# Float16 halves for the scores of a pooled-attention MLP kernel, and DMA-turned queries and values

## The chip, the core and the metric

The kernel runs on one core of one Trainium2 chip. The metric is the device time of one execution in microseconds, lower is better. TensorE (PE) multiplies matrices, VectorE (DVE), ScalarE (ACT) and GpSimd (POOL) work on tiles of 128 partitions, and SyncE (SP) issues all DMAs of this kernel, in order, on one queue. Each engine works through its own list of instructions in the order in which the program wrote them, and waits at semaphores for the others.

## The reference

Four batches of 12288 queries of 128 channels; `kv` is 384 x 32 positions of 128 channels per batch. Keys and values are the same pooled matrix.

```python
kv_pool = kv.reshape(B, H // r, r, W // r, r, C).mean(axis=(2, 4))   # r = 4: 768 positions
kv_flat = kv_pool.reshape(B, -1, C) @ w_sr
k = v = kv_flat
s = scale * (q @ k.transpose(0, 2, 1)); s = s - s.max(-1, keepdims=True)
a = np.exp(s); a /= a.sum(-1, keepdims=True) + 1e-09
x = (a @ v).reshape(B * N, C)
h = x @ w_in                                  # 128 -> 2048
g = 0.5 * h * (1.0 + erf(h / sqrt(2)))
out = g @ w_out                               # 2048 -> 128
```

## The kernel before

**Tiles.** The 49152 tokens are 96 tiles of 512, 24 to a batch. A tile has four token blocks `c` of 128. To keep float32 precision on 16-bit or reduced matmuls, each operand is split into a high and a low half, and three products (high-high, high-low, low-high) are added in PSUM.

**Stages of a tile t**, with the lines that the profile names:

- `q_load`; `q_planes` (L307) copies the upper and lower 16 bits of q apart, `q_turn` lets a DMA transpose these two planes, `q_join` (L321) puts them together, `q_high` (L335) and `q_low` (L341) make the two float32r halves. All on GpSimd in the steady loop but `q_high`, which is on VectorE.
- `score` (L352): for each block, six matmuls of 384 columns (three products, two halves of the 768 keys) into the one buffer `ps_s`. `evac` (L363) copies it to SBUF times -1.0 and takes the minimum.
- `exps` (L409, ScalarE), `recips` (L422, L425), then `attn` per block: `attn_hi` (L429) and `attn_lo` (L433) on VectorE, and `attn_turn` (L442), a DMA transpose into `aT`, of which there is one buffer.
- `av` (L471): 18 matmuls of 512 columns with the value halves. `x_out` (L481, L482) splits the result.
- For each of 16 blocks `f` of the hidden layer: `mlp_in` (L490 to L492), `gelu` (L504, and L506 for each pair, which makes `gh`), `rest` (L510, VectorE, makes `gl` for a pair), `mlp_out` (L521 to L523), six steps later. The pair's float32 result `g` has two buffers, so the gelu of a pair waits for the `rest` of the pair two before.
- The output is copied into 16-bit planes (`o_turn`, L307), turned by DMA, joined (`o_join`) and stored.

**Order.** Nothing is scheduled by a planner: the program writes the order by hand. `START` lists the work of the start and of tile 0. After it a double loop over tile i and step f mixes the MLP of tile i with the attention of tiles i+1 to i+3: `q_load(i+3)` at f=1, blocks 1 to 3 of `attn(i+1)` at f=1, 3, 5, `score` and `evac` of tile i+2 at f=3, 6, 9, q's planes and turn at f=5, its join at f=8, `exps(i+2)` and q's halves at f=10, `av(i+1)` at f=10 to 12, `score(i+3, 0)` at f=13, `recips(i+2)` and block 0 at f=15, and a `rest` at every even f. Within one f the order of the source holds.

**Keys and values.** Each batch's keys are summed, turned on TensorE (`kv_turn`, L201), multiplied by `w_sr` (`kv_key`) and split (`kv_key_low`, L220). When all are there, each channel's largest gives a scale; the scaled keys are turned back on TensorE (`kv_val`, L286) and split into the value halves. `mlp_scale` needs the largest over the partitions: a matmul with ones (L249) and a reduction.

**Weights.** `w_max`, `w_scale` and `w_split` make float16 halves of both weights in the start, with scales per partition.

Of the kernel before, what the change touches and what calls it, by code (L numbers as in the profile page):

```python
# [23 lines left out]
    ("q_planes", 0, "act"), ("kv_load", 3), ("kv_load", 4), ("kv_load", 5), ("q_load", 1),  # L24
    ("q_turn", 0), ("kv_load", 6), ("kv_load", 7), ("q_planes", 1, "pool"), ("kv_load", 8),
    ("kv_load", 9), ("kv_load", 10), ("kv_load", 11), ("wi_load", 0), ("wi_load", 1), ("q_turn", 1),
    ("q_load", 2), ("q_load", 3), ("wo_load", 0), ("wi_load", 2), ("wo_load", 1), ("wi_load", 3),
# [1 line left out]
    ("kv_sum", 1, 1), ("kv_sum", 2, 0), ("kv_sum", 2, 1), ("kv_key_low", 0), ("kv_turn", 1),
    ("kv_key", 1), ("kv_turn", 2), ("q_join", 0, "act"), ("q_high", 0, "act"), ("q_low", 0),  # L30
# [6 lines left out]
    ("kv_turn", 5), ("w_max", 2), ("w_max", 3), ("w_scale", 0), ("kv_key", 5), ("kv_key_low", 5), ("evac_half", 0, 3, 0), ("w_split", 0, 2),
    ("kv_max",), ("w_split", 1, 0), ("q_join", 1, "act"), ("w_split", 0, 3),
    ("score_half", 0, 0, 1), ("evac_half", 0, 0, 1), ("exp", 0, 0), ("score_half", 0, 1, 1),
    ("evac_half", 0, 1, 1), ("evac_half", 0, 2, 0), ("exp", 0, 1), ("score_half", 0, 2, 1),  # L40
    ("evac_half", 0, 2, 1), ("kv_scale", 0), ("exp", 0, 2), ("recips", 0, 0, 2), ("kv_scale", 1),
    ("score_half", 0, 3, 1), ("q_high", 1, "pool"), ("q_low", 1), ("q_join", 2, "pool"),
    ("kv_mul",), ("mlp_scale",), ("recips", 0, 2, 1), ("evac_half", 0, 3, 1), ("attn_hi", 0, 0, "act"),
    ("attn_hi", 0, 1, "act"), ("exp", 0, 3), ("attn_hi", 0, 2, "act"), ("attn_lo", 0, 0),
    ("attn_turn", 0, 0), ("attn_lo", 0, 1), ("attn_turn", 0, 1), ("recips", 0, 3, 1),
    ("w_split", 1, 1), ("attn_hi", 0, 3, "act"), ("attn_lo", 0, 2), ("attn_turn", 0, 2),
    ("attn_lo", 0, 3), ("attn_turn", 0, 3), ("q_planes", 3, "act"), ("w_max", 4),
# [7 lines left out]
    ("score_half", 1, 3, 1), ("score", 1, 2), ("mlp_in", 0, 0), ("evac_half", 1, 1, 1),
    ("exp", 1, 1), ("evac", 1, 2), ("exp", 1, 2), ("evac_half", 1, 3, 0), ("evac_half", 1, 3, 1),
    ("exp", 1, 3), ("q_high", 2, "act"), ("q_low", 2), ("w_split", 2, 1), ("recips", 1, 0, 4),
    ("w_split", 2, 2), ("attn_hi", 1, 0, "act"), ("attn_lo", 1, 0), ("attn_turn", 1, 0),
    ("q_turn", 3), ("attn_hi", 1, 1, "act"), ("gelu", 0, 0), ("w_split", 2, 3), ("score", 2, 0),
    ("mlp_in", 0, 1), ("attn_lo", 1, 1), ("evac", 2, 0), ("gelu", 0, 1), ("w_split", 5, 0),  # L60
    ("attn_turn", 1, 1), ("mlp_in", 0, 2), ("gelu", 0, 2), ("w_split", 5, 1), ("rest", 0, 0),
    ("w_split", 5, 2), ("w_split", 5, 3), ("score", 2, 1), ("mlp_in", 0, 3),
    ("attn_hi", 1, 3, "act"), ("gelu", 0, 3), ("attn_hi", 1, 2, "act"), ("w_split", 3, 0),
    ("mlp_in", 0, 4), ("w_split", 3, 1), ("evac", 2, 1), ("rest", 0, 1), ("attn_lo", 1, 3),
    ("attn_lo", 1, 2), ("attn_turn", 1, 2), ("gelu", 0, 4), ("mlp_in", 0, 5), ("gelu", 0, 5),
    ("w_split", 3, 2), ("attn_turn", 1, 3), ("w_split", 3, 3), ("mlp_out", 0, 0), ("mlp_in", 0, 6),
    ("mlp_out", 0, 1), ("gelu", 0, 6), ("score", 2, 2), ("rest", 0, 2), ("evac", 2, 2),
    ("mlp_in", 0, 7), ("gelu", 0, 7), ("w_split", 6, 0), ("mlp_out", 0, 2), ("mlp_in", 0, 8),
    ("mlp_in", 0, 9), ("gelu", 0, 8), ("rest", 0, 3), ("w_split", 6, 1), ("w_split", 6, 2),
    ("w_split", 6, 3), ("gelu", 0, 9), ("mlp_out", 0, 3), ("mlp_out", 0, 4), ("mlp_in", 0, 10),  # L70
    ("score", 2, 3), ("q_join", 3, "dve"), ("evac", 2, 3), ("mlp_out", 0, 5), ("av", 1, 0),
    ("gelu", 0, 10), ("exp", 2, 2), ("w_split", 7, 0), ("q_high", 3, "pool"), ("q_low", 3),
    ("exp", 2, 1), ("exp", 2, 0), ("exp", 2, 3), ("mlp_in", 0, 11), ("av", 1, 1), ("mlp_in", 0, 12),
    ("av", 1, 2), ("gelu", 0, 11), ("gelu", 0, 12), ("mlp_in", 0, 13), ("mlp_out", 0, 6),
    ("w_split", 7, 1), ("w_split", 7, 2), ("rest", 0, 4), ("x_out", 1), ("gelu", 0, 13),
    ("mlp_out", 0, 7), ("mlp_out", 0, 8), ("rest", 0, 5), ("mlp_out", 0, 9), ("score", 3, 0),
    ("mlp_in", 0, 14), ("gelu", 0, 14), ("mlp_in", 0, 15), ("recips", 2, 0, 4),
    ("attn_hi", 2, 0, "dve"), ("rest", 0, 6), ("attn_lo", 2, 0), ("gelu", 0, 15), ("evac", 3, 0),
# [5 lines left out]
def pooled_attention_mlp(  # L84
# [145 lines left out]

    def kv_scale(b, step):
        if step == 0:
            e2 = small.tile([P, 1], I32, tag="e2", name=f"e2_{b}")
# [3 lines left out]
            nc.vector.tensor_scalar(
                e2, st["mx", b].bitcast(I32), 0x7F800000, None, op0=ALU.bitwise_and
            )
# [533 lines left out]
```

## Time and profile before

| | |
|---|---|
| three runs | 2953.82, 2955.94, 2957.46 us; median 2955.94 |
| profiled execution | 2959.45 us, its span 2957.7 us |
| granted TensorE clock | 0.99 |
| busy | PE 2828.8, ACT 2535.7, DVE 2294.4, POOL 992.6 us |

The span is what the profiler saw from the first to the last instruction; the execution's time is a little longer. In the rows below, a timeline row gives start and length in us, engine, line, operation, output <- inputs, shapes and count, and in brackets how long the engine stood idle before it and what released it. A group row gives, after the count, the busy time in us and the mean of one in ns, then the idle time before them. A row of the stretches gives start and end, and for PE, PE's weight loads, DVE, ACT and POOL the busy time with the number of instructions. Names lose their buffer numbers, so `g` is any buffer of `g`.

### The profile page before, as it was taken

Reading aid. Unit: us, or ns where it says so; the run is one execution under the profiler, and the core shown is the slowest. Engines: PE = TensorE matmul, PEld = TensorE weight load, DVE = VectorE, ACT = ScalarE, POOL = GpSimd, SP = SyncE. Lnnn points to the kernel's source line nnn. Section 1 sums busy time; section 2 is a strip of 40 time slices with the busy share of each in tenths; the row PEclk is TensorE's granted clock in tenths of the full one; section 3 lists DMA queues with packets and bytes.
Section 4 is the critical chain, followed back from the end, with each engine's and each line's share of the span. In section 5 each row is a group of like instructions: output and inputs, shape, how many; then the busy total and the mean of one; then the engine's idle time right before and its main releaser. Section 6 shows DMA issues by size and latency. Waiting matters only on the chain.

```text
span 2957.7 us, 37444 instructions
## 1 busy us (share of the span) xinstructions
PE 2828.8 (96%) x13412; PEld 1479.2 (50%) x13412; DVE 2294.4 (78%) x3043; ACT 2535.7 (86%) x3429; POOL 992.6 (34%) x1009
## 2 busy tenths in 40 slices
...
GB/s 189 66 95 113 94 113 95 94 85 86 93 100 107 102 115 89 104 75 93 86 97 97 116 106 100 107 86 89 82 97 86 93 86 97 86 93 86 93 84 56
DMA packets 848443, 283.31 MB, mean 96 GB/s; under 512 B 808576, under 2 KB 811008, under 8 KB 848256
## 3 DMA queue, kind: packets, MB, share of 16 engines
...
q8 instruction: 105, 1.72, 0.2%
...
## 4 chain that ended last, share of the span: by engine, by line
PE 56%; DVE 22%; ACT 10%; issue 4%; DMA 4%; POOL 0%; SPq 0%; ACTq 0%; DVEq 0%
PE px L471 10%; DVE gl L510 9%; PE s L352 7%; PE po L521 7%; PE po L522 6%; PE po L523 6%; PE h L490 6%; PE h L492 6%; PE h L491 6%; DVE a L433 5%; DVE a L429 4%; ACT g L504 4%; DMA aT<-a 3%; ACT sn L409 3%; DVE sn L363 2%
## 5 line engine op out<-in xcount | busy, mean ns | idle before, releaser
L504 ACT ACTIVATE g<-h,hs 128x512 f32<-128x512 f32 x1536 | 1003.3, 680 | 327.1 <-DVE gl L510 160.7
L510 DVE SCALAR_TENSOR_TENSOR gl<-g,gs,gh 128x1024 f16<-128x1024 f32 x768 | 1027.4, 1347 | 129.9 <-ACT gh L506 125.9
L506 ACT ACTIVATE gh<-g,gs 128x1024 f16<-128x1024 f32 x768 | 882.1, 1149 | 24.9
L307 POOL COPY q_u<-q 128x512 uint16<-128x512 uint16 x188 | 189.4, 1035 | 1332.1 <-DMA q<-in_q_dram 1315.3
L522 PE MATMUL po<-gl,wo_h 128*128 128x512 f16 x1536 | 583.4, 380 | 8.9 <-DVE gl L510 8.9
L521 PE MATMUL po<-gh,wo_h 128*128 128x512 f16 x1536 | 586.4, 382 | 2.1 <-ACT oT L528 2.1
L490 PE MATMUL h<-xh,wi_h 128*128 128x512 f16 x1536 | 585.1, 381 | 0.1
L491 PE MATMUL h<-xl,wi_h 128*128 128x512 f16 x1536 | 583.8, 380 | 0.0
L492 PE MATMUL h<-xh,wi_l 128*128 128x512 f16 x1536 | 583.6, 380 | 0.0
L523 PE MATMUL po<-gh,wo_l 128*128 128x512 f16 x1536 | 583.3, 380 | 0.0
L433 DVE SCALAR_TENSOR_TENSOR a<-sn,r,a 128x768 f16<-128x768 f32 x384 | 426.3, 1111 | 13.3
L471 PE MATMUL px<-aT,vh 128*128 128x512 f16 x1140 | 342.9, 383 | 45.4 <-issue 32.7
L363 DVE TENSOR_SCALAR_CACHE_REDUCE sn<-s 128x768 f32<-128x768 f32 x378 | 358.6, 949 | 21.2 <-PE s L352 20.8
L409 ACT ACTIVATE sn<-sn,nm 128x768 f32<-128x768 f32 x384 | 354.5, 924 | 20.6 <-DVE nm L403 17.8
L481 DVE TENSOR_SCALAR xh<-px,xs 128x512 f16<-128x512 f32 x96 | 72.1, 751 | 366.2 <-PE px L471 366.2
L321 POOL COPY qT<-q_v 128x512 uint16<-128x512 uint16 x186 | 219.1, 1220 | 210.3 <-DMA q_v<-q_u 210.3
L352 PE MATMUL s<-kh,qh 128*128 128x384 f32 x756 | 263.8, 430 | 8.6 <-DVE sn L363 4.5
L429 DVE TENSOR_SCALAR a<-sn,r 128x768 f16<-128x768 f32 x376 | 254.7, 677 | 3.8 <-DVE r L425 0.5
L523 PEld LDWEIGHTS <-wo_l 128*128 128x128 f16 x1536 | 150.5, 98 | 191.1 <-issue 10.8
L521 PEld LDWEIGHTS <-wo_h 128*128 128x128 f16 x1536 | 150.2, 98 | 188.8 <-issue 44.8
L490 PEld LDWEIGHTS <-wi_h 128*128 128x128 f16 x1536 | 150.6, 98 | 186.5 <-issue 17.6
L492 PEld LDWEIGHTS <-wi_l 128*128 128x128 f16 x1536 | 150.7, 98 | 182.3 <-issue 1.9
...
## 6 DMA issues: line engine op xcount, KB each, us to landing
...
aT<-a SPq DMA_TRANSPOSE x384, 3.8
...
q_v<-q_u SPq DMA_TRANSPOSE x96, 3.6
o_v<-o_u SPq DMA_TRANSPOSE x95, 3.4
```

What stands on the lines that cost most here:

```text
L352: nc.tensor.matmul(ps[:, n, :KH], lhs[:, cs], rhs[:, n * KH : (n + 1) * KH], start=rhs is kh and lhs is qh, stop=lhs is ql,)
L433: nc.vector.scalar_tensor_tensor(a[:, 1, :], st.pop(("s", t, c)), st["r", t][:, c : c + 1], a[:, 0, :], op0=ALU.mult, op1=ALU.subtract,)
L471: nc.tensor.matmul(ps, v[:, k, :], aT[:, :, o + k, :], start=k == 0 and i == 0, stop=k == KB - 1 and i == 2,)
L490: nc.tensor.matmul(ps, wi_h[:, fs], xh, start=True, stop=False)
L491: nc.tensor.matmul(ps, wi_h[:, fs], xl, start=False, stop=False)
L492: nc.tensor.matmul(ps, wi_l[:, fs], xh, start=False, stop=True)
L504: nc.scalar.activation(g[:, e, :], ps, AF.Gelu, scale=st["hs", b])
L506: nc.scalar.mul(gh, g, st["gs", b])
L510: nc.vector.scalar_tensor_tensor(gl, st["g", t, p], st["gs", t // TPB], st["gh", t, p], op0=ALU.mult, op1=ALU.subtract)
L521: nc.tensor.matmul(ps, wo_h[:, f, :], gh[:, e, :], start=f == 0, stop=False)
L522: nc.tensor.matmul(ps, wo_h[:, f, :], gl[:, e, :], start=False, stop=False)
L523: nc.tensor.matmul(ps, wo_l[:, f, :], gh[:, e, :], start=False, stop=f == FB - 1)
```

## The change

- **Queries.** `q_planes`, `q_join`, `q_high` and `q_low` go. At f=4 `q_max` reduces each token's absolute largest on VectorE, `q_scale` makes a power of two and its inverse from it (three small operations), and `q_split` on GpSimd multiplies by the inverse, copies to float16 and subtracts: two float16 halves. At f=8 `q_turn` has the DMA transpose the halves, and `q_sigma` (VectorE) makes the factor that undoes the scales of token and keys. The halves go straight into the matmuls.
- **Keys.** One scale per batch: `kv_max`, and `kv_bound` in four steps (a diagonal, the matmul with ones, the reduction and the scales). `kv_high` and `kv_low` make float16 halves of all keys. `kv_key_low` and `kv_mul` go.
- **Scores.** The matmuls read float16 halves; `evac` multiplies by `q_sigma`'s column instead of -1.0.
- **Values.** `kv_val` is one DMA transpose of the key halves; the transposes on TensorE and the split of the values go.
- **MLP scales.** `mlp_scale` is three small operations per batch; the largest over the partitions is taken once, in `w_scale`, which is now in three steps. `w_split`'s third step can run on ScalarE.
- **Start.** `START` is written anew: all of the first batch's keys come first, then the four blocks of tile 0's scores, and most weight splits after the first `av`.

The core of the diff:

```diff
+    def q_max(t):
+        st["qm", t] = small.tile([P, CH], F32, tag="qm", name=f"qm_{t}")
+        nc.vector.tensor_reduce(
+            st["qm", t], st["q", t], axis=AX.X, op=ALU.max, apply_absolute_value=True)
+    def q_scale(t):
+        m = st.pop(("qm", t))
...
+        nc.vector.tensor_scalar_max(m, m, 2.0**-90)
+        nc.vector.tensor_scalar(
+            st["qe", t], m.bitcast(I32), 0x7F800000, None, op0=ALU.bitwise_and)
+        nc.vector.tensor_scalar(
+            st["qi", t], st["qe", t], -1.0, float(268 << 23), op0=ALU.mult, op1=ALU.add)
+    def q_split(t, eng=nc.gpsimd):
+        x = st.pop(("q", t))
+        u = qs.tile([P, 2, CH, C], F16, tag="u", name=f"q_{t}_u")
+        i = st.pop(("qi", t)).bitcast(F32).unsqueeze(2).to_broadcast([P, CH, C])
+        eng.tensor_tensor(x, x, i, op=ALU.mult)
+        eng.tensor_copy(u[:, 0], x)
+        eng.tensor_tensor(u[:, 1], x, u[:, 0], op=ALU.subtract)
     def q_turn(t):
-        st["qv", t] = turn(qs, st.pop(("qu", t)), f"q_{t}")
+        u = st.pop(("qu", t))
+        v = qs.tile([P, 2, CH, P], F16, tag="v", bufs=2, name=f"q_{t}_v")
+        nc.sync.dma_start_transpose(
+            v.rearrange("p e c d -> p (e c) d"), u.rearrange("p e c d -> p (e c d)"))
+        st["qT", t] = v[:, 0], v[:, 1]
+    def q_sigma(t):
+        st["sg", t] = small.tile([P, CH], F32, tag="sg", name=f"sg_{t}")
+        nc.vector.tensor_scalar_mul(
+            st["sg", t], st.pop(("qe", t)).bitcast(F32), st["ks", t // TPB])
...
-            s.rearrange("p (n k) -> p n k", n=2), st.pop(("ps", t, c))[:, :, :KH], -1.0, None,
+            s.rearrange("p (n k) -> p n k", n=2), st.pop(("ps", t, c))[:, :, :KH],
+            st["sg", t][:, c : c + 1], None,
...
+    def kv_high(b, n=0, parts=1, mul=nc.vector.tensor_scalar_mul):
+        if n == 0:
+            st["k", b] = keys.tile([P, 2, KEYS], F16, tag="k", name=f"k_{b}")
+        s = slice(n * KEYS // parts, (n + 1) * KEYS // parts)
+        mul(st["k", b][:, 0, s], st["kT", b][:, s], st["kinv", b])
+    def kv_low(b, n=0, parts=1):
...
+        nc.vector.scalar_tensor_tensor(
+            k[:, 1, s], st["kT", b][:, s], st["kinv", b], k[:, 0, s],
+            op0=ALU.mult, op1=ALU.subtract)
+    def kv_val(b):
+        st["v", b] = keys.tile([P, 2 * KB, C], F16, tag="v", name=f"v_{b}")
+        nc.sync.dma_start_transpose(st["v", b], st["k", b].rearrange("p n k -> p (n k)"))
...
-        at(i1, 11, kv_scale, b, 0)
-        at(i1, 11, kv_scale, b, 1)
-        at(i1, 11, kv_mul, b)
-        at(i1 + 1, 9, mlp_scale, b)
-        at(i1 + 1, 9, out_scale, b)
-        at(i1 + 1, 11, kv_val, b, 0, 4, ps_t, "ps_t")
...
+        at(i1, 11, kv_bound, b, 0)
+        at(i1 + 1, 2, kv_bound, b, 1)
+        at(i1 + 1, 11, kv_bound, b, 2)
+        at(i1 + 1, 11, kv_bound, b, 3)
+        at(i1 + 1, 12, mlp_scale, b)
+        at(i1 + 1, 12, out_scale, b)
+        at(i1 + 2, 11, kv_high, b)
+        at(i1 + 2, 12, kv_low, b)
+        at(i1 + 3, 11, kv_val, b)
...
-                if i + 3 < NT and f == 5:
-                    q_planes(i + 3)
-                    q_turn(i + 3)
+                if i + 3 < NT and f == 4:
+                    q_max(i + 3)
+                    q_scale(i + 3)
+                    q_split(i + 3)
+                if i + 3 < NT and f == 8:
+                    q_turn(i + 3)
+                    q_sigma(i + 3)
...
-                if f == 8 and i + 3 < NT:
-                    q_join(i + 3)
-                if f == 10 and i + 3 < NT:
-                    q_high(i + 3)
-                    q_low(i + 3)
```

In the new `START`, after the loads and the keys of the first batch:

```python
    ("kv_turn", 4), ("kv_key", 4), ("kv_turn", 5), ("kv_key", 5), ("kv_max", 1), ("kv_bound", 0),
    ("w_split", 0, 0), ("kv_bound", 1), ("w_max", 0), ("kv_bound", 2), ("kv_high", 0),
    ("kv_high", 1), ("kv_low", 0), ("kv_bound", 3), ("q_sigma", 0), ("kv_low", 1), ("kv_val",),
    ("score_half", 0, 0, 0), ("score_half", 0, 1, 0), ("score_half", 0, 2, 0),
...
    ("w_scale", 0, 0), ("w_scale", 0, 1), ("w_split", 0, 1), ("w_split", 0, 2, "act"),
    ("w_scale", 0, 2), ("mlp_scale",), ("w_split", 0, 3), ("q_sigma", 1), ("score", 1, 0),
    ("evac", 1, 0), ("score_half", 1, 1, 0), ("score_half", 1, 1, 1), ("w_split", 1, 0),
    ("av_first", 0, 0), ("av_first", 0, 1), ("w_split", 1, 1), ("w_split", 1, 2, "act"),
    ("av_first", 0, 2), ("av_first", 0, 3), ("exp", 1, 0), ("w_split", 1, 3), ("x_out", 0),
```

More of the change, by code (lines that the diff above doesn't have):

```diff
@@ L23 @@
     ("q_load", 0), ("kv_load", 0), ("kv_load", 1), ("w_sr",), ("kv_load", 2),
[L24 to L27, printed above, removed]
+    ("q_max", 0), ("q_scale", 0), ("q_split", 0), ("kv_load", 3), ("kv_load", 4), ("kv_load", 5),
@@ L28 @@
+    ("q_load", 1), ("kv_load", 6), ("q_turn", 0), ("kv_load", 7), ("kv_load", 8), ("kv_load", 9),
+    ("kv_load", 10), ("kv_load", 11), ("wi_load", 0), ("wi_load", 1), ("wi_load", 2),
+    ("wi_load", 3), ("q_load", 2), ("wo_load", 0), ("wo_load", 1),
     ("kv_sum", 0, 0), ("kv_sum", 0, 1), ("kv_sum", 1, 0), ("kv_turn", 0), ("kv_key", 0),
[L29 to L30 removed]
@@ L37 @@
[L37 to L47, printed above, removed]
@@ L55 @@
[L55 to L66, printed above, removed]
@@ L67 @@
[L67 to L78, printed above, removed]
@@ L79 @@
-    ("attn_turn", 2, 0), ("w_split", 7, 3),
+    ("kv_sum", 1, 1), ("kv_sum", 2, 0), ("kv_sum", 2, 1), ("kv_turn", 1), ("kv_key", 1),
+    ("q_max", 1), ("q_scale", 1), ("q_split", 1), ("kv_turn", 2), ("kv_sum", 3, 0),
+    ("kv_sum", 3, 1), ("kv_key", 2), ("kv_max", 0), ("kv_sum", 4, 0), ("kv_turn", 3),
+    ("kv_key", 3), ("kv_sum", 4, 1), ("q_turn", 1), ("kv_sum", 5, 0), ("kv_sum", 5, 1),
+    ("kv_turn", 4), ("kv_key", 4), ("kv_turn", 5), ("kv_key", 5), ("kv_max", 1), ("kv_bound", 0),
+    ("w_split", 0, 0), ("kv_bound", 1), ("w_max", 0), ("kv_bound", 2), ("kv_high", 0),
@@ new lines @@
+    ("score_half", 1, 3, 1), ("exp", 1, 2), ("evac_half", 1, 3, 0), ("evac_half", 1, 3, 1),
+    ("exp", 1, 3), ("recips", 1, 0, 4), ("attn_hi", 1, 0, "dve"), ("attn_lo", 1, 0),
+    ("attn_turn", 1, 0), ("gelu", 0, 0), ("mlp_in", 0, 1), ("gelu", 0, 1), ("w_max", 4),
+    ("w_max", 5), ("w_max", 6), ("w_max", 7), ("w_scale", 1, 0), ("mlp_in", 0, 2),
+    ("w_scale", 1, 1), ("gelu", 0, 2), ("rest", 0, 0), ("w_split", 4, 0), ("w_split", 4, 1),
+    ("w_scale", 1, 2), ("out_scale",), ("w_split", 4, 2, "dve"), ("w_split", 4, 3),
@@ new lines @@
+    ("mlp_in", 0, 3), ("gelu", 0, 3), ("rest", 0, 1), ("w_split", 2, 0), ("w_split", 2, 1),
+    ("w_split", 2, 2, "dve"), ("w_split", 2, 3), ("q_sigma", 2), ("score", 2, 0), ("mlp_in", 0, 4), ("evac", 2, 0),
+    ("gelu", 0, 4), ("mlp_in", 0, 5), ("gelu", 0, 5), ("rest", 0, 2), ("attn_hi", 1, 1, "dve"),
+    ("attn_lo", 1, 1), ("attn_turn", 1, 1), ("mlp_out", 0, 0), ("mlp_in", 0, 6),
+    ("mlp_out", 0, 1), ("gelu", 0, 6), ("w_split", 5, 0), ("w_split", 5, 1), ("score", 2, 1),
+    ("evac", 2, 1), ("w_split", 5, 2, "dve"), ("w_split", 5, 3), ("mlp_in", 0, 7),
@@ new lines @@
+    ("gelu", 0, 7), ("mlp_out", 0, 2), ("rest", 0, 3), ("attn_hi", 1, 2, "dve"),
+    ("attn_lo", 1, 2), ("attn_turn", 1, 2), ("mlp_out", 0, 3), ("w_split", 3, 0), ("w_split", 3, 1),
+    ("w_split", 3, 2, "dve"), ("w_split", 3, 3), ("mlp_in", 0, 8), ("gelu", 0, 8),
+    ("attn_hi", 1, 3, "dve"), ("attn_lo", 1, 3), ("attn_turn", 1, 3), ("mlp_in", 0, 9),
+    ("gelu", 0, 9), ("mlp_out", 0, 4), ("rest", 0, 4), ("score", 2, 2), ("evac", 2, 2),
+    ("mlp_out", 0, 5), ("q_max", 3), ("q_scale", 3), ("q_split", 3), ("q_turn", 3),
@@ new lines @@
+    ("q_sigma", 3), ("mlp_in", 0, 10), ("gelu", 0, 10), ("w_split", 6, 0), ("w_split", 6, 1),
+    ("mlp_in", 0, 11), ("gelu", 0, 11), ("mlp_out", 0, 6), ("rest", 0, 5), ("w_split", 6, 2, "dve"),
+    ("w_split", 6, 3), ("score", 2, 3), ("evac", 2, 3), ("mlp_out", 0, 7),
+    ("mlp_in", 0, 12), ("gelu", 0, 12), ("exp", 2, 0), ("exp", 2, 1), ("exp", 2, 2), ("exp", 2, 3),
+    ("av", 1, 0), ("w_split", 7, 0), ("w_split", 7, 1), ("mlp_in", 0, 13), ("av", 1, 1),
+    ("gelu", 0, 13), ("mlp_out", 0, 8), ("rest", 0, 6), ("av", 1, 2), ("w_split", 7, 2, "dve"),
@@ L80 @@
+    ("w_split", 7, 3), ("x_out", 1), ("mlp_in", 0, 14), ("gelu", 0, 14), ("mlp_out", 0, 9),
+    ("recips", 2, 0, 4), ("attn_hi", 2, 0, "dve"), ("attn_lo", 2, 0), ("attn_turn", 2, 0),
+    ("mlp_in", 0, 15), ("gelu", 0, 15), ("score", 3, 0), ("evac", 3, 0),
 ]
@@ L321, in join @@
             copy(w[:, :, e], v[:, e, :, :].rearrange("p c d -> p (c d)"))
-    def q_planes(t, *copy):
-        st["qu", t] = planes(qs, st.pop(("q", t)).rearrange("p c d -> p (c d)"), f"q_{t}", *copy)
-    def q_turn(t):
-        st["qv", t] = turn(qs, st.pop(("qu", t)), f"q_{t}")
-    def q_join(t, *copy):
-        st["qj", t] = qs.tile([P, T], F32, tag="qT", name=f"qT_{t}")
-        join(st.pop(("qv", t)), st["qj", t], *copy)
-    def q_high(t, copy=nc.vector.tensor_copy):
-        qh = qs.tile([P, T], F32R, tag="qh", name=f"qh_{t}")
-        copy(qh, st["qj", t])
-        st["qh", t] = qh
@@ L385, in score_half @@
         for i, (lhs, rhs) in enumerate(((qh, kh), (ql, kh), (qh, kl))):
-            nc.tensor.matmul(ps, lhs[:, cs], rhs[:, ks], start=i == 0, stop=i == 2)
+            nc.tensor.matmul(ps, lhs[:, c], rhs[:, ks], start=i == 0, stop=i == 2)
         st["s", t, c, n] = ps
```

268 lines of the change are left out of this document (138 added, 130 removed).

## The prediction

> **What bounds the kernel now.** I read the page first: busy shares and the chain that ended last.
>
> ```profile
> PE 2828.8 (96%) x13412; PEld 1479.2 (50%) x13412; DVE 2294.4 (78%) x3043; ACT 2535.7 (86%) x3429; POOL 992.6 (34%) x1009
> ...
> PE 56%; DVE 22%; ACT 10%; issue 4%; DMA 4%; POOL 0%; SPq 0%; ACTq 0%; DVEq 0%
> ```
>
> By the shares TensorE is the bound, but a quarter of the chain runs through VectorE and the transposes. So I read one quiet tile in the timelines, first VectorE from one `recips` (L422) to the next.
>
> ```profile
> 2403.01 0.16 DVE L422 TENSOR_SCALAR r<-sum 128x4 f32<-128x4 f32 x1
> ...
> 2409.87 0.62 DVE L429 TENSOR_SCALAR a<-sn,r 128x768 f16<-128x768 f32 x1
> 2410.52 1.24 DVE L433 SCALAR_TENSOR_TENSOR a<-sn,r,a 128x768 f16<-128x768 f32 x1
> 2411.69 1.63 DVE L510 SCALAR_TENSOR_TENSOR gl<-g,gs,gh 128x1024 f16<-128x1024 f32 x1
> 2413.24 0.96 DVE L429 TENSOR_SCALAR a<-sn,r 128x768 f16<-128x768 f32 x1
> 2414.24 1.24 DVE L433 SCALAR_TENSOR_TENSOR a<-sn,r,a 128x768 f16<-128x768 f32 x1
> 2415.40 0.94 DVE L363 TENSOR_SCALAR_CACHE_REDUCE sn<-s 128x768 f32<-128x768 f32 x1
> 2416.28 0.08 DVE L363 DVE_READ_ACCUMULATOR sn<-s 128x1 f32 x1
> 2416.28 2.92 DVE L510 SCALAR_TENSOR_TENSOR gl<-g,gs,gh 128x1024 f16<-128x1024 f32 x2
> ...
> 2432.52 0.16 DVE L422 TENSOR_SCALAR r<-sum 128x4 f32<-128x4 f32 x1
> ```
>
> No row from 2403.01 on names a wait: for 14.6 us, to the end of the first L510 of the last pair (about 2417.5), VectorE runs back to back. ScalarE and TensorE hang on that stretch:
>
> ```profile
> 2417.65 1.26 ACT L504 ACTIVATE g<-h,hs 128x512 f32<-128x512 f32 x2 [1.79 <-DVE gl L510]
> ...
> 2420.69 1.28 ACT L409 ACT_TABLE_LOAD   x1
> ...
> 2430.13 1.15 ACT L506 ACTIVATE gh<-g,gs 128x1024 f16<-128x1024 f32 x1
> ```
>
> ```profile
> 2418.67 0.38 PE L492 MATMUL h<-xh,wi_l 128*128 128x512 f16 x1
> 2419.37 0.59 PE L471 MATMUL px<-aT,vh 128*128 128x512 f16 x2 [0.33 <-DMA aT<-a]
> ```
>
> The gelu of f=8 needs one of the two `g` buffers, so it waits 1.79 us for that L510. From there ScalarE is busy (gelus, a table load, four exps) until `gh` at 2431.28, which releases the L510 ahead of the next `recips`. So there is a ring with no slack: 14.6 us of VectorE, 13.7 us of ScalarE, 1.2 us of L510, together 29.5. TensorE is nearly as slow but stands at `av` until the last attention transpose has landed: it has slack, the ring has none. First and last steady `recips`, 93 tiles apart:
>
> ```profile
> 160.49 0.16 DVE L422 TENSOR_SCALAR r<-sum 128x4 f32<-128x4 f32 x1
> ...
> 2901.99 0.16 DVE L422 TENSOR_SCALAR r<-sum 128x4 f32<-128x4 f32 x1
> ```
>
> (2901.99 - 160.49)/93 = 29.48 us a tile. What is put into that VectorE stretch is paid 93 times.
>
> GpSimd matters because it stretches VectorE there:
>
> ```profile
> 2410.05 2.19 POOL L307 COPY q_u<-q 128x512 uint16<-128x512 uint16 x2 [15.02 <-DMA q<-in_q_dram]
> 2412.95 1.72 POOL L307 COPY o_u<-oT 128x512 uint16<-128x512 uint16 x2 [0.71 <-ACT oT L528]
> ```
>
> Beside these copies L433 takes 1.24 us twice, L429 0.96, L510 1.63. The same lines without such a neighbour take 1.02, 0.62 and 1.28 (second fence below). That is 0.22 + 0.35 + 0.34 + 0.22 = 1.13 us a tile of sharing.
>
> **The change, part by part.** Rows that price it:
>
> ```profile
> L580 DVE TENSOR_REDUCE wm<-wi 128x1 f32<-128x512 f32 x4 | 2.7, 684 | 5.9 <-DMA wi<-in_moe_w_in_dram 5.9
> L237 DVE TENSOR_SCALAR e<-mx 128x1 int32<-128x1 int32 x4 | 0.6, 154 | 0.1
> L335 DVE CAST qh<-qT 128x512 fp32r<-128x512 f32 x92 | 38.6, 420 | 8.5 <-POOL qT L321 8.5
> L481 DVE TENSOR_SCALAR xh<-px,xs 128x512 f16<-128x512 f32 x96 | 72.1, 751 | 366.2 <-PE px L471 366.2
> L294 DVE CAST vh<-pv 128x512 f16<-128x512 f32 x4 | 2.8, 693 | 13.8 <-PE pv L286 13.8
> ```
>
> ```profile
> 2404.08 1.02 DVE L433 SCALAR_TENSOR_TENSOR a<-sn,r,a 128x768 f16<-128x768 f32 x1
> 2405.02 1.28 DVE L510 SCALAR_TENSOR_TENSOR gl<-g,gs,gh 128x1024 f16<-128x1024 f32 x1
> ```
>
> 1. *`q_max` and `q_scale`, new on VectorE at f=4.* In program order they stand between `attn(i+1, 2)` and the `rest` of f=4, inside the stretch. One reduction of 128x512 is priced by L580 (0.68), three operations on 128x4 by L237 (0.154, issued about 0.19 apart): 0.68 + 3 x 0.19 = 1.25 us a tile. Queued behind: `rest`, `attn(i+1, 3)`, its transpose, the `rest` that frees `g`. Nothing covers them. `q_max` also waits for the load of q; copy L307 shows q landed 7.0 us after `recips`, VectorE gets there at 8.7 (1.24 from 2410.52): covered by 1.7 us.
>
> 2. *`q_high` (0.42) leaves VectorE* at f=10, where VectorE waits for `px` (366.2 us over the run): gain 0. `q_sigma` at f=8 (0.15) comes after the L510 that releases ScalarE: 0.
>
> 3. *The evacuations take a scale per token instead of -1.0.* L481, with a scale from a tile, takes 0.751, L294, with none, 0.693, for the same 512 PSUM columns: +0.06, and two stand in the stretch: +0.12. Ends 0 and +0.12; a gain is excluded, since an operand is added.
>
> 4. *GpSimd:* the two q copies, two joins and `q_low` go; `q_split` comes, a multiply, a copy and a subtraction, released by `q_scale`, so just when VectorE starts L510, L429, L433, L363, L510. No row shows it, so I bound it. The nearest row for a two-input GpSimd operation beside VectorE:
>
> ```profile
> 122.00 2.28 DVE L510 SCALAR_TENSOR_TENSOR gl<-g,gs,gh 128x1024 f16<-128x1024 f32 x1
> ```
> ```profile
> 121.89 1.31 POOL L636 TENSOR_TENSOR wt<-wt 128x512 f32<-128x512 f32 x1 [1.68 <-ACT gh L506]
> ```
>
> The L510 ended 1.08 us after L636 did: it stood still, losing 1.00. So in the stretch: the multiply waits for L510, then holds up L429 (1.0); the copy holds up L433 as copies do now (0.22); the subtraction falls on L363, which reads PSUM, with 0.15 left on L510: 1.37, against 1.13 now, +0.24. Ends: -1.13, if VectorE never lets GpSimd in, and +1.9, if all three stop it in full (three times 1.0 less 1.13). I take +0.24, nearest to the L636 row, of the same kind and size.
>
> For the copy a page speaks otherwise. The Trainium skill, "SBUF — State Buffer", section "Who interferes with whom", says that a GpSimd instruction holds the port pair it shares with VectorE for its whole length and that the other "fully blocks". The L636 row agrees; L307's rows (0.22 to 0.35 for copies of about 1 us) do not. By the rule a copy of 0.7 us (its cast on GpSimd in the start took 708 ns) would cost some 0.2 us more a tile, an estimate, and the sum would be 19 us higher. I keep the measured rows.
>
> 5. *GpSimd and SP order.* `q_split` is now ahead of `o_turn`'s copies, and SP issues q's transpose after the last `aT` and `o_turn` instead of ahead of the last `aT`. q then lands near f=12 and is needed at f=13; `o_join` follows at f=11. Both are covered by the longer tile, 0. If the cover went, TensorE would wait for q, within its slack of item 6.
>
> 6. *TensorE: float16 scores.*
>
> ```profile
> 1503.13 0.38 PE L492 MATMUL h<-xh,wi_l 128*128 128x512 f16 x1
> 1503.16 0.70 PE L352 MATMUL s<-kh,qh 128*128 128x384 f32 x2
> ...
> 1504.40 0.39 PE L521 MATMUL po<-gh,wo_h 128*128 128x512 f16 x1
> ```
>
> A 512-column matmul advances by 0.216, so six of 384 would take 0.97; from 1503.35 to 1504.40 they took 1.05. Gain 0.08 x 4 = 0.33 us a tile, on an engine that waits: worth 0, it only lengthens the wait at `av`. Without the ring it would be 31 us.
>
> 7. *Per batch.* Key lows and value splits leave VectorE at f=11, `kv_high` and `kv_low` come there, all in its wait for `px`: 0. The value transposes go from TensorE to the DMA, one more beside 4 per tile: 0. `mlp_scale` loses its matmul, for which TensorE stood still:
>
> ```profile
> PE um_ps L249 <- DVE um_d L247: 15.5, 4, 7.0
> ```
>
> Less the 7.0 in the start, 8.5 us over three batches; `kv_bound`'s matmul comes a third of a tile after its input: -8.5.
>
> 8. *The start.* The values no longer wait for the weights' scales, so the first MLP matmul comes earlier, but what follows is VectorE's list:
>
> ```profile
> 72.00:90.00 18.00, 11.59 (x100) 8.13 (x97) 17.56 (x33) 10.62 (x17) 11.59 (x9) 0.91 0.01 1
> 90.00:110.00 20.00, 13.94 (x59) 7.79 (x60) 19.79 (x26) 14.96 (x21) 11.16 (x8) 0.91 0.50 93
> 110.00:130.00 20.00, 13.59 (x53) 6.68 (x52) 19.46 (x25) 12.73 (x20) 11.78 (x9) 0.83 0.00 0
> ```
>
> VectorE (third number) is full from 72 to 130. In come four times 1.25 and five attention multiplies of 0.62 that ScalarE did; out go key lows, value splits, two join copies and two weight steps, about as much. I take 0, ends -8 and +8 (the 18 us of the first row, give or take half).
>
> Sum: 1.25 + 0.12 + 0.24 = 1.61 us a tile x 93 = +150; -8.5; 0. The profiled execution's 2959.45 becomes 3101. The median of the runs is 3.5 lower: 3097, and I say 3095.
>
> **The rivals.**
>
> *TensorE sets the period after all* (faster, the other side). For it: 96% busy, and q's reduction would fit VectorE's 22% idle. Then 31 + 8.5 come off: 2916. It decides if the stretch grows by under 0.1 us. Against: the stretch has no gap, and TensorE waits at `av`.
>
> *VectorE keeps GpSimd out.* The q copies leave the stretch and nothing takes their place: 1.25 + 0.12 - 1.13 = +0.24 a tile, +22 - 8.5: 2970. For it: whichever starts first holds up the other, and VectorE's list has no gap in which GpSimd could start; against: L636.
>
> *TensorE's clock falls.* Its wait would grow from 0.50 to 0.50 + 1.61 + 0.33 = 2.4 us a tile, and after such a wait:
>
> ```profile
> 1825.91 0.96 PE L471 MATMUL px<-aT,vh 128*128 128x512 f16 x2 [2.32 <-issue]
> ...
> 1828.38 0.63 PE L521 MATMUL po<-gh,wo_h 128*128 128x512 f16 x1
> 1828.80 0.63 PE L522 MATMUL po<-gl,wo_h 128*128 128x512 f16 x1
> ```
>
> a matmul takes 0.42 instead of 0.22 for some 3 us. That or full stops cost 0.7 us a tile more: 3160.
>
> *Another order or landing cancels the effect:* no change, 2956.
>
> **How the numbers follow.** Forecast 0.62, clock or full stops 0.14, GpSimd kept out 0.12, TensorE bound 0.08, no change 0.04. About 0.2% (6 us) is what a measurement can tell. Slower 0.84 (0.62 + 0.14 + most of 0.12), same 0.06, faster 0.10. The forecast's own range is 3040 to 3140; with GpSimd kept out and the costlier case 2960 to 3165.
>
> **What would show it.** `recips` 31.1 us apart; in the stretch a reduction and three short operations of 1.25 us, an L429 near 1.6; waits of 2 us at `av`; scores 0.97 us for six; no wait at L249's matmul. Wrong if `recips` come 29.2 apart or closer, or if VectorE shows a gap before `q_max`.

## The result, and the profile after

The changed kernel takes 3061.62 us (median of four runs, 3058.22 to 3065.32) against 2956.7 for the one before on the same chip: 1.0356 times as long, with a 95% interval of 1.0338 to 1.0374. 3095 was predicted (1.047 times), slower in the right way but a third too much. The profiled spans are 3063.5 and 2957.7 us, 105.8 apart. Page of the changed kernel, busy shares and the chain that ended last:

```profile
PE 2811.9 (92%) x13390; PEld 1311.8 (43%) x13390; DVE 2443.4 (80%) x3379; ACT 2513.5 (82%) x3414; POOL 909.3 (30%) x825
...
DVE 48%; ACT 26%; PE 13%; issue 7%; DMA 5%; SPq 0%; DVEq 0%; ACTq 0%
```

TensorE fell from 96% busy to 92%, and from 56% of the chain to 13%: VectorE and ScalarE now carry it, as a ring through both would. One quiet tile on VectorE, from one `recips` (now L443) to the next; `attn_hi` is L450, `attn_lo` L454, `evac` L383, `rest` L531, `q_max` L324, `q_scale` L333 to L337, `q_sigma` L361:

```profile
2515.22 0.16 DVE L443 TENSOR_SCALAR r<-sum 128x4 f32<-128x4 f32 x1
...
2522.13 0.61 DVE L450 TENSOR_SCALAR a<-sn,r 128x768 f16<-128x768 f32 x1
2522.78 1.02 DVE L454 SCALAR_TENSOR_TENSOR a<-sn,r,a 128x768 f16<-128x768 f32 x1
2523.71 0.68 DVE L324 TENSOR_REDUCE qm<-q 128x4 f32<-128x512 f32 x1
2524.43 0.17 DVE L333 TENSOR_SCALAR qm<-qm 128x4 f32<-128x4 f32 x1
2524.63 0.17 DVE L334 TENSOR_SCALAR qe<-qm 128x4 int32<-128x4 int32 x1
2524.91 0.17 DVE L337 TENSOR_SCALAR qi<-qe 128x4 int32<-128x4 int32 x1
2524.98 1.28 DVE L531 SCALAR_TENSOR_TENSOR gl<-g,gs,gh 128x1024 f16<-128x1024 f32 x1
2526.18 1.40 DVE L450 TENSOR_SCALAR a<-sn,r 128x768 f16<-128x768 f32 x1
2527.61 1.24 DVE L454 SCALAR_TENSOR_TENSOR a<-sn,r,a 128x768 f16<-128x768 f32 x1
2528.78 1.00 DVE L383 TENSOR_SCALAR_CACHE_REDUCE sn<-s,sg 128x768 f32<-128x768 f32 x1
2529.72 1.27 DVE L531 SCALAR_TENSOR_TENSOR gl<-g,gs,gh 128x1024 f16<-128x1024 f32 x1
2530.91 0.57 DVE L361 TENSOR_SCALAR sg<-qe,ks 128x4 f32<-128x4 f32 x1
...
2545.95 0.16 DVE L443 TENSOR_SCALAR r<-sum 128x4 f32<-128x4 f32 x1
```

The stretch from 2515.22 to the end of the L531 that frees `g` (2530.91, where L361 begins) is 15.69 us, again without a gap; before it was 14.47 (L510 ends some 0.17 ahead of the gelu that it releases, as L531 does here, so at 2417.48). From L324 to the next L531, 2523.71 to 2524.98, it holds the new 1.27 us. GpSimd works right behind:

```profile
2525.16 2.00 POOL L345 TENSOR_TENSOR q<-q,qi 128x512 f32<-128x512 f32 x1 [19.18 <-DVE qi L337]
2527.23 0.82 POOL L346 CAST q_u<-q 128x512 f16<-128x512 f32 x1
2528.12 1.74 POOL L347 TENSOR_TENSOR q_u<-q,q_u 128x512 f16<-128x512 f32 x1
2529.82 2.20 POOL L305 COPY o_u<-oT 128x512 uint16<-128x512 uint16 x2
```

Beside the multiply L450 takes 1.40 instead of 0.61 to 0.62, beside the cast and the first part of the subtraction L454 takes 1.24 instead of 1.02; beside the subtraction L383 and L531 lose nothing. The sharing in the stretch is 0.78 + 0.22 = 1.00 us, less than the 1.13 before. ScalarE hangs on the end of the stretch as before, and TensorE now stands at the scores, not at `av` (ScalarE's timeline, TensorE's timeline, and TensorE's waits with total, times and longest):

```profile
2531.08 1.26 ACT L525 ACTIVATE g<-h,hs 128x512 f32<-128x512 f32 x2 [2.28 <-DVE gl L531]
```
```profile
2529.85 1.14 PE L372 MATMUL s<-k,q_v 128*128 128x384 f16 x6 [1.60 <-DVE sn L383]
2530.82 0.38 PE L542 MATMUL po<-gh,wo_h 128*128 128x512 f16 x1
```
```profile
PE s L372 <- DVE sn L383: 133.7, 89, 2.1
PE px L492 <- DMA aT<-a: 40.5, 86, 2.1
```

Six score matmuls advance by 2530.82 - 2529.85 = 0.97 us, as forecast. Third and last whole-tile `recips` of the run:

```profile
170.23 0.16 DVE L443 TENSOR_SCALAR r<-sum 128x4 f32<-128x4 f32 x1
...
3007.56 0.17 DVE L443 TENSOR_SCALAR r<-sum 128x4 f32<-128x4 f32 x1
```

Between them lie 92 tiles, not the 93 that the prediction divided by. That gives (3007.56 - 170.23) / 92 = 30.84 us a tile; the kernel before had (2901.99 - 160.49) / 92 = 29.80. So the 105.8 us are 92 x 1.04 = 95.8 in the tiles, 170.23 - 160.49 = 9.7 in the start, and 0.3 behind the last `recips`.

### The profile page after: what moved, and what is told of

The parts are those of the page before. It is cut to its first block, busy times and chain, and to the rows that moved or that the text cites. A ratio compares the mean times of both kernels' runs of the same rounds, so it can differ in the third digit from the quotient of the medians.

```text
span 3063.5 us, 37495 instructions
## 1 busy us (share of the span) xinstructions
PE 2811.9 (92%) x13390; PEld 1311.8 (43%) x13390; DVE 2443.4 (80%) x3379; ACT 2513.5 (82%) x3414; POOL 909.3 (30%) x825
## 4 chain that ended last, share of the span: by engine, by line
DVE 48%; ACT 26%; PE 13%; issue 7%; DMA 5%; SPq 0%; DVEq 0%; ACTq 0%
DVE gl L531 17%; DVE a L454 10%; DVE a L450 9%; ACT g L525 9%; ACT sn L430 7%; DVE sn L383 5%; ACT gh L527 5%; PE px L492 5%; DMA aT<-a 4%; ACT L525 3%; ACT L430 3%; DVE qm L324 2%; PE po L542 1%; PE po L543 1%; PE po L544 1%
## 5 line engine op out<-in xcount | busy, mean ns | idle before, releaser
L525 ACT ACTIVATE g<-h,hs 128x512 f32<-128x512 f32 x1536 | 989.9, 679 | 458.1 <-DVE gl L531 386.6
L531 DVE SCALAR_TENSOR_TENSOR gl<-g,gs,gh 128x1024 f16<-128x1024 f32 x768 | 1023.2, 1333 | 157.7 <-ACT gh L527 147.6
L345 POOL TENSOR_TENSOR q<-q,qi 128x512 f32<-128x512 f32 x96 | 189.1, 1969 | 1640.6 <-DVE qi L337 1640.5
L372 PE MATMUL s<-k,q_v 128*128 128x384 f16 x2268 | 435.4, 329 | 133.7 <-DVE sn L383 133.7
L492 PE MATMUL px<-aT,v 128*128 128x512 f16 x1710 | 420.2, 382 | 42.6 <-DMA aT<-a 40.5
L454 DVE SCALAR_TENSOR_TENSOR a<-sn,r,a 128x768 f16<-128x768 f32 x384 | 415.4, 1082 | 15.0 <-ACT a L450 1.6
L383 DVE TENSOR_SCALAR_CACHE_REDUCE sn<-s,sg 128x768 f32<-128x768 f32 x378 | 380.9, 1008 | 1.8 <-PE s L372 1.5
L372 PEld LDWEIGHTS <-q_v 128*128 128x128 f16 x2268 | 222.5, 98 | 338.7 <-issue 164.4
L450 DVE TENSOR_SCALAR a<-sn,r 128x768 f16<-128x768 f32 x381 | 309.2, 811 | 3.4
L492 PEld LDWEIGHTS <-v 128*128 128x128 f16 x1710 | 162.3, 98 | 268.4 <-issue 52.5
L319 POOL COPY o<-o_v 128x512 uint16<-128x512 uint16 x190 | 138.5, 773 | 347.5 <-DMA o_v<-o_u 342.3
```

What stands on the lines that cost most here:

```text
L372: nc.tensor.matmul(ps[:, n, :KH], lhs[:, c], rhs[:, n * KH : (n + 1) * KH], start=rhs is kh and lhs is qh, stop=lhs is ql,)
L454: nc.vector.scalar_tensor_tensor(a[:, 1, :], st.pop(("s", t, c)), st["r", t][:, c : c + 1], a[:, 0, :], op0=ALU.mult, op1=ALU.subtract,)
L492: nc.tensor.matmul(ps, v[:, w, :], aT[:, :, o + k, :], start=k == 0 and i == 0, stop=k == KB - 1 and i == 2,)
L525: nc.scalar.activation(g[:, e, :], ps, AF.Gelu, scale=st["hs", b])
L531: nc.vector.scalar_tensor_tensor(gl, st["g", t, p], st["gs", t // TPB], st["gh", t, p], op0=ALU.mult, op1=ALU.subtract)
```

## The experiments

Times are medians; a ratio is to the kernel before on the same chip, with its interval. "Tile" is the distance of two `recips` in a quiet tile, one in which no batch's keys are made (where such tiles differ, a frequent one), "mean" that over 92 tiles.

**Does TensorE matter?** `x2_pe_more` does the first of the three score products twice.

```diff
+        for n in range(2):
+            nc.tensor.matmul(
+                ps[:, n, :KH], qh[:, c], kh[:, n * KH : (n + 1) * KH], start=True, stop=True,
+            )
```

> The changed kernel with more TensorE work: the first product of each score is done twice (two matmuls of 384 columns more per score, 0.32 us, four scores a tile; the second writes over the first). The ring theory: TensorE has some 2 us of slack a tile, so the median moves by less than 15 us (3060 to 3075). Rival, TensorE sets the period (92% busy): 1.3 us x 92 = 119 us more, 3180.

3061.63 us, 1.0351 [1.0336, 1.0365]; tile 30.73. TensorE was given 112.5 us of work and the time did not move:

```profile
PE 2924.4 (96%) x14146; PEld 1384.9 (45%) x14146; DVE 2443.8 (80%) x3379; ACT 2514.7 (82%) x3414; POOL 907.4 (30%) x825
```

So what float16 saves on TensorE could not show either.

**The reduction alone.** `x3_before_qmax` is the kernel before with an unused `q_max` and `q_scale` at f=4.

```diff
+                if i + 3 < NT and f == 4:
+                    q_extra(i + 3)   # the reduction and the three small operations
```

> The kernel before with one part of the change added: q_max and q_scale of tile i+3 at f=4 on VectorE, their results unused; q's planes, join and float32r halves as before. The ring theory: 1.27 us more in the stretch, a quiet tile goes from 29.5 to 30.75, and 92 tiles at some 1.0 us over their present mean make 3050 (3030 to 3070), nearly all of the loss. Rival, the loss comes from GpSimd's split holding VectorE up, from the scale operand or from the start: less than 30 us, under 2990.

3050.72 us, 1.0313 [1.0299, 1.0328]; tile 30.60, mean 30.82. Four VectorE instructions a tile bring 92 us of the loss, with float32 scores and without the rest of the change. (30.60 against 29.51 is 1.09, not 1.27: GpSimd's copies hold VectorE up for different times from tile to tile here, and quiet tiles take 30.3 to 31.1. Averages over all tiles follow below.)

**The scale operand.** `x4_evac_const` puts a constant into `evac` (the token scales are left out).

```diff
-            st["sg", t][:, c : c + 1], None,
+            -(2.0**-32), None,
```

> The changed kernel with a constant instead of the scale per token in the full evacuations (L383), so the scales of queries and keys are not undone there. The ring theory: L383 takes 0.95 instead of 1.01 us, two of them stand in the stretch, 0.12 us x 92 = 11 us less: 3050. Rival, the operand is free where it matters: 3061, no change. Rival, all four count: 22 us less, 3040.

3050.14 us, 1.031 [1.0296, 1.0325]; tile 30.64, so 0.10 a tile against the 0.12 that was put on it. L383 falls from 1.00 to 0.95. The 11.5 us and the 92 of `x3_before_qmax` make 103 of the 105; what is left, the start among it, nearly cancels.

**The reduction out of the stretch.** `x1_q_early` loads q one tile earlier and does all of q's preparation at f=11.

```diff
-                if i + 3 < NT and f == 4:
-                    q_max(i + 3)
...
+                if i + 4 < NT and f == 11:
+                    q_max(i + 4)
...
```

> The changed kernel with one thing moved: q_max, q_scale and q_split of a tile are issued one tile earlier, at f=11, where VectorE waits some 4 us for px, and q's load one tile earlier too. The same work, the same engines. The ring theory: the stretch from recips to the L531 that frees g loses the 1.27 us of the reduction and its three small operations and the hold-up of L450 (0.78), gets back some sharing with the output's copies; recips come 29.0 to 29.3 us apart instead of 30.74, median near 2905 (2885 to 2930), below both kernels. Rival, the float16 path itself is slow (its matmuls, its transposes, the scale operand): stays at 3050 to 3065. Rival, the moved work collides with the L531s before recips, which are in the ring too: 2980 to 3040.

2918.38 us, 0.9865 [0.9851, 0.9879]: the change is now faster than the kernel before. Tile 29.04, mean 29.24. VectorE and GpSimd:

```profile
2425.07 0.16 DVE L443 TENSOR_SCALAR r<-sum 128x4 f32<-128x4 f32 x1
...
2434.76 0.97 DVE L450 TENSOR_SCALAR a<-sn,r 128x768 f16<-128x768 f32 x1
2435.77 1.24 DVE L454 SCALAR_TENSOR_TENSOR a<-sn,r,a 128x768 f16<-128x768 f32 x1
...
2439.06 0.22 DVE L361 TENSOR_SCALAR sg<-qe,ks 128x4 f32<-128x4 f32 x1
...
2442.92 0.68 DVE L324 TENSOR_REDUCE qm<-q 128x4 f32<-128x512 f32 x1
```
```profile
2434.62 1.58 POOL L305 COPY o_u<-oT 128x512 uint16<-128x512 uint16 x2 [14.98 <-ACT oT L549]
```

The reduction now stands in VectorE's wait for `px`. The stretch is 13.99 us; the output's plane copies, no longer queued behind `q_split`, come into it and cost 0.35 + 0.22.

**GpSimd's multiply.** `x5_no_mul` leaves it out (the queries' scaling with it).

```diff
-        eng.tensor_tensor(x, x, i, op=ALU.mult)
```

> The changed kernel without GpSimd's multiply of the queries by their inverse scale (the queries' scaling is left out). GpSimd's 2.00 us beside VectorE's two attention operations are gone. Theory (the hold-up of VectorE beside GpSimd lies in the stretch that bounds the tile): L450 goes from 1.40 back to about 0.65 to 1.0, the tile from 30.74 to 30.0 to 30.5, the kernel to 2995 to 3040. Rival (GpSimd only moves forward: the copies of the halves and of the output then fall on the two attention operations and cost as much): the tile stays at 30.6 to 30.8 and the kernel at 3050 to 3062.

3088.83 us, 1.0435 [1.0413, 1.0457]: 27 us slower than the changed kernel, beyond either expectation. Without the multiply `q_split` waits only for q's load, and its subtraction and the output's copies behind it now run beside `q_scale`:

```profile
2513.89 0.42 DVE L333 TENSOR_SCALAR qm<-qm 128x4 f32<-128x4 f32 x1
2514.34 0.52 DVE L334 TENSOR_SCALAR qe<-qm 128x4 int32<-128x4 int32 x1
2514.89 0.52 DVE L337 TENSOR_SCALAR qi<-qe 128x4 int32<-128x4 int32 x1
```

Operations on four elements lose 0.25 to 0.35 each, as much as one of 768 does. The stretch is 15.78 us, the tile 30.85: the sharing only changed its place. Many other tiles take 31.3 (mean 31.10); in most of these the stretch is 16.24, so they too lie on the ring. That q's load now sets when GpSimd starts, and so which operations it holds up, would explain why tiles differ; this is not shown.

**The split alone late.** `x11_split_late` keeps `q_max` and `q_scale` at f=4 and puts only `q_split` at f=11.

```diff
...
+                if i + 4 < NT and f == (11 if i == 1 else 4):
+                    q_max(i + 4)
+                    q_scale(i + 4)
+                if i + 4 < NT and f == 11:
+                    q_split(i + 4)
```

> The changed kernel with the queries loaded one tile earlier and only GpSimd's split of them moved to the end of the tile; the reduction and its three small operations stay in VectorE's stretch. It divides the 1.70 us a tile that the fully early queries gained (30.74 to 29.04). Theory: 1.25 us of that was VectorE's own reduction and scale, and 0.45 the hold-up beside GpSimd, so the tile goes to 30.2 to 30.4, the mean to 30.3 to 30.5 and the kernel to 3010 to 3035. Rival (the hold-up was worth all of it or nothing): under 3000, or 3055 to 3062.

3103.9 us, 1.0506 [1.0491, 1.0522], slower than all others. The edit did not do what was meant: GpSimd has nothing else queued between the output's copies and f=11, so the multiply, which needs nothing but `qi`, started right behind them in the stretch; only the cast waited. But the copies fell differently from tile to tile, and so one trace holds both cases. Two tiles that follow each other, on VectorE and GpSimd:

```profile
2458.21 0.16 DVE L443 TENSOR_SCALAR r<-sum 128x4 f32<-128x4 f32 x1
...
2469.18 0.97 DVE L450 TENSOR_SCALAR a<-sn,r 128x768 f16<-128x768 f32 x1
2470.18 1.24 DVE L454 SCALAR_TENSOR_TENSOR a<-sn,r,a 128x768 f16<-128x768 f32 x1
...
2473.48 0.22 DVE L361 TENSOR_SCALAR sg<-qe,ks 128x4 f32<-128x4 f32 x1
...
2488.52 0.16 DVE L443 TENSOR_SCALAR r<-sum 128x4 f32<-128x4 f32 x1
...
2498.22 0.49 DVE L337 TENSOR_SCALAR qi<-qe 128x4 int32<-128x4 int32 x1
2498.62 1.70 DVE L531 SCALAR_TENSOR_TENSOR gl<-g,gs,gh 128x1024 f16<-128x1024 f32 x1
2500.24 1.39 DVE L450 TENSOR_SCALAR a<-sn,r 128x768 f16<-128x768 f32 x1
...
2504.74 0.23 DVE L361 TENSOR_SCALAR sg<-qe,ks 128x4 f32<-128x4 f32 x1
...
2519.78 0.16 DVE L443 TENSOR_SCALAR r<-sum 128x4 f32<-128x4 f32 x1
```
```profile
2468.25 2.36 POOL L305 COPY o_u<-oT 128x512 uint16<-128x512 uint16 x2 [17.97 <-ACT oT L549]
2470.58 1.74 POOL L345 TENSOR_TENSOR q<-q,qi 128x512 f32<-128x512 f32 x1
...
2498.07 1.17 POOL L305 COPY o_u<-oT 128x512 uint16<-128x512 uint16 x2 [16.84 <-ACT oT L549]
2499.20 2.01 POOL L345 TENSOR_TENSOR q<-q,qi 128x512 f32<-128x512 f32 x1
```

In the first tile sharing costs 0.35 + 0.22, in the second 0.32 + 0.42 + 0.77: the stretch grows from 15.27 to 16.22, by 0.95, and the tile from 30.31 to 31.26, by 0.95. Eleven tiles of the run take 30.31, within the 30.2 to 30.4 that was expected of all.

**The ring as a law.** The stretch and the tile, from these rows and the same two lines of the other traces:

| | stretch | tile | difference |
|---|---|---|---|
| `x1_q_early` | 13.99 | 29.04 | 15.05 |
| before | 14.47 | 29.51 | 15.04 |
| `x11_split_late`, 2458 | 15.27 | 30.31 | 15.04 |
| `x4_evac_const` | 15.60 | 30.64 | 15.04 |
| changed | 15.69 | 30.73 | 15.04 |
| `x5_no_mul` | 15.78 | 30.85 | 15.07 |
| `x11_split_late`, 2488 | 16.22 | 31.26 | 15.04 |

In these tiles the stretch is passed on one to one, whatever is in it. Taken in all 92 tiles of ten of the traces, the difference is never under 15.03 us: the ring is a floor. But a tile can be longer than the ring. Counted are the tiles within 0.05 us of 15.04, the other columns are means over the 92 tiles:

| | stretch | difference | tile | tiles on the ring |
|---|---|---|---|---|
| before | 14.27 | 15.53 | 29.80 | 52 |
| `x3_before_qmax` | 15.59 | 15.22 | 30.82 | 84 |
| changed | 15.69 | 15.15 | 30.84 | 78 |
| `x9_before_early` | 13.54 | 16.03 | 29.57 | 0 |

The quiet tile of the kernel before, with its 14.47, has one of the longer stretches. In 40 of the kernel's 92 tiles something else than the ring set the time. 32 of these lie in three runs of eleven tiles in which the next batch's keys are made; there TensorE is mostly either busy throughout or stands 1 to 3 us at `av`. So the change put 15.69 - 14.27 = 1.42 us a tile into the stretch, and 15.53 - 15.15 = 0.38 of it does not show in the time: it was hidden where the tile had been longer than the ring, or made up for by work saved there. In `x3_before_qmax`, which has the old work per batch, 1.32 went in and 0.30 was hidden.

The table of single tiles also divides what `x1_q_early` gained: 15.27 - 13.99 = 1.28 us is VectorE's reduction and scale, at equal sharing, and 15.69 - 15.27 = 0.42 is sharing.

**What float16 is worth at equal places.** `x9_before_early` is the kernel before with its queries early in the same manner.

```diff
...
-                    q_planes(i + 3)
...
+                if i + 4 < NT and f == 11:
+                    q_planes(i + 4)
```

> The kernel before, scores in float32, with the queries' plane copies taken one tile earlier and moved to VectorE's idle part. It has none of the change's steps. Theory (the stretch on VectorE sets the tile): of its 29.50 the copies and their sharing leave, 0.35 to 0.57 us: 28.9 to 29.2 a tile and 2905 to 2940 in all, as much as the changed kernel with its queries early (2918), so float16 scores are worth nothing here beside the placement. Rival (TensorE's floor with float32 scores, 28.7 busy a tile, takes over): 29.4 to 29.5 and 2950 to 2960.

2938.25 us, 0.9929 [0.9909, 0.9949], tile 28.87. The theory's numbers come about by luck, and its last words do not hold: 0.9929 against 0.9865 of `x1_q_early` leaves float16 some 19 us. The mechanism is the rival's, at a lower floor than it named: no tile of the run lies on the ring, which with a stretch of 13.64 would allow 28.68, and TensorE has no idle time in the quiet tile (below). The quiet tile is no longer than in `x1_q_early`, but the mean is 29.57 against 29.24: the tiles with a batch's keys and values are the long ones.

**GpSimd's copies out of the stretch.** `x10_out_act` is `x1_q_early` with the output's plane copies on ScalarE, at f=5.

```diff
-        st["ov", t] = turn(op, planes(op, st.pop(("oT", t)), f"o_{t}"), f"o_{t}")
+        st["ov", t] = turn(op, planes(op, st.pop(("oT", t)), f"o_{t}", nc.scalar.copy), f"o_{t}")
...
-                if f == 6 and 0 <= i - 1 < NT - 1:
+                if f == 5 and 0 <= i - 1 < NT - 1:
```

> The changed kernel with its queries taken early (29.04 a tile, 2918), and the two copies of the output's planes, GpSimd's 1.58 us beside VectorE's attention operations, on ScalarE one step earlier. Theory: the hold-up of about 0.5 us leaves the stretch, the ring falls to about 28.5, which is also about where TensorE is full: 2865 to 2895. Rival (ScalarE is now in the way, or TensorE takes over at once): the tile stays at 28.9 to 29.3, 2905 to 2940.

2890.44 us, 0.9767 [0.9748, 0.9787], the fastest of all. Stretch 13.41, tile 28.49. One quiet tile of `x9_before_early`, then of `x10_out_act`: start and end, then TensorE's busy time first:

```profile
2505.82:2534.69 28.87, 28.87 (x140) 15.18 (x139) 22.16 (x31) 26.16 (x36) 8.10 (x9) 1.00 0.45 92
```
```profile
2517.51:2546.00 28.49, 28.49 (x140) 13.50 (x138) 22.86 (x34) 27.03 (x38) 4.17 (x5) 1.00 0.45 93
```

TensorE is busy without a break in both, and the two tiles differ by 28.87 - 28.49 = 0.38 us, close to the 0.33 that item 6 forecast for float16 scores. In `x10_out_act` the ring, 13.41 + 15.04 = 28.45, lies only 0.04 lower: the two bounds nearly meet there.

**The start.** `x7_start_act` gives tile 1's four attention multiplies back to ScalarE; `x12_start_const` also takes constant scales for tiles 1 to 3.

```diff
-("attn_hi", 1, 0, "dve")
+("attn_hi", 1, 0, "act")    # and 1, 2, 3
```
```diff
-            "q_max": q_max, "q_scale": q_scale, "q_turn": q_turn, "q_sigma": q_sigma,
+            "q_max": lambda t: q_max(t) if t == 0 else None,
+            "q_scale": lambda t: q_scale(t) if t == 0 else q_const(t),
+            "q_turn": q_turn, "q_sigma": q_sigma,
...
```

> The changed kernel with tile 1's four attention multiplies on ScalarE in the start, where they were before the change. Theory (the start is 9.7 us longer because VectorE has 7 us more work up to tile 2's reciprocal): the third reciprocal comes 3 to 6 us earlier than 170.2 and the kernel ends at 3055 to 3059. Rival (the start is set by ScalarE's and TensorE's chain): the third reciprocal stays within 1 us or comes later, 3061 to 3068. The tiles stay at 30.74.

> The changed kernel with ScalarE doing tile 1's four attention multiplies in the start, and constant scales for the queries of tiles 1 to 3 in place of VectorE's reduction and scale: 8 to 9 us of VectorE's work are gone from the start, as much as it had gained over the kernel before. Theory (VectorE's work sets the start): the third reciprocal of a whole tile, at 170.2 in the changed kernel, comes at 161 to 166, and the kernel ends at 3052 to 3057. Rival (the weights' splits, late on GpSimd, hold TensorE and set it): the third reciprocal at 168 to 171, and the kernel at 3057 to 3063.

`x7_start_act`: 3057.35 us, 1.0334 [1.0312, 1.0356], third reciprocal at 170.04: the rival's place for the reciprocal, though the time lies in the theory's range. `x12_start_const`: 3060.04, 1.0363 [1.0345, 1.038], third reciprocal at 166.82, between the two. Taking away 8 to 9 us of VectorE's work gives 3.4 back, and the totals can't be told from the changed kernel's. In the changed kernel TensorE also stands 13 us at the low halves of the output weights between 70 and 170 us (13.4 in `x12_start_const`); the kernel before has no wait named so, but 8.9 us on `gl` there:

```profile
PE po L544 <- POOL wo_l L683: 13.0, 3, 5.4
```

Whether that wait makes the other 6 us was not tried; it stays open.

## Why the prediction was right, and what was off

1. *The bound.* A ring of VectorE and ScalarE that TensorE only follows: right for the changed kernel, as `x2_pe_more` and the tables show. "The ring has none" and "paid 93 times" were too strong for the kernel before: only 52 of its 92 tiles lay on the ring. The miscount of 93 for 92 hid that the mean before was 29.80, 0.3 above the quiet tile. (The 14.6 us of VectorE run to the gelu's start; to the end of the L510 it is 14.47.)
2. *`q_max` and `q_scale`, +1.25:* 1.27 in the rows, 1.28 between traces; `x3_before_qmax` shows 1.32 in the mean stretch, 1.02 of it in the time.
3. *The scale operand, +0.12:* 0.10 by `x4_evac_const`.
4. *Sharing, +0.24:* mis-sized. From quiet tile to quiet tile it measured 1.00 - 1.13 = -0.13. Over all tiles, many of which had less sharing before than the one shown, it is 1.42 - 1.27 - 0.10 = +0.05, and 0.19 x 92 = 17 us of the forecast did not come. The multiply costs L450 0.78, not the 1.00 that was taken over from L510; the cast 0.22 as forecast; the subtraction nothing in the stretch, as it stands beside L383, and its 0.15 on L510 did not come. The Trainium skill, "SBUF — State Buffer", section "Who interferes with whom", says that a VectorE instruction with at most one SBUF input, outside the two-port modes, does not contend with GpSimd; L383, which reads PSUM, agrees with 1.00 beside the subtraction.

   Of the full block, which the prediction weighed for the cast by the same section and set aside, the rows show more than was read from them. L450, L454 and L531 (L429, L433 and L510 before) lost the time from their own beginning to the end of the GpSimd instruction then running, less 0.20 to 0.25 us. L636 ended 1.20 after L510 began, which lost 1.00; the multiply ended 0.98 after L450 began, which lost 0.78; the cast ended 0.44 after L454 began, which lost 0.22. In the kernel before, plane copies ended 0.55 or 0.44 after such a beginning and cost 0.35 or 0.23 (medians). So the small losses are the remainders of a full block and not a milder kind of sharing, and a loss follows from how much of GpSimd's instruction is left.
5. *Queue order, 0:* no wait of the scores for q is among TensorE's waits.
6. *Float16 worth 0:* right in this kernel; 0.38 a tile once the ring is shorter. But TensorE's slack went to the scores (133.7 us, behind the later `evac`) and not to `av` (40.5).
7. *Per batch, -8.5:* the work itself was near this, but the prediction had no term for the cover that a longer ring gives. What a tile takes beyond its stretch fell from 15.53 to 15.15, 35 us over 92 tiles. 28 of the 35 are gone already in `x3_before_qmax`, where the batch's work is the old one: the longer ring covers what had made tiles longer. Some 7 are left for the change.
8. *The start, 0:* +9.7 us, just outside the bound of 8; VectorE's added work explains about a third.

Together: 131 us more in the stretch, 35 less beyond it and 9.7 more in the start make, within rounding, the 105.8; forecast were 148, 8.5 and 0. So the direction and the cause were right, and 3095 was 33 too high mainly because of sharing (17) and the cover (28); that the start put 9.7 back was luck. Of the rivals, GpSimd was not kept out (L450 lost 0.78), TensorE did not set the period of the changed kernel, and its clock stayed at 0.99.
